# Sparse attention and a gated feed-forward on one core: the first blocks' keys and queries in 1 KB runs, turned by identity matmuls, with constant matmuls in the first waits

## The chip, the core and the metric

The program runs on one core of one Trainium2 chip. A core has a matrix engine (TensorE; PE in the profile, and PEld for its weight loads), a vector engine (VectorE, DVE), a scalar engine (ScalarE, ACT), a general engine (GpSimd, POOL) and a queue engine (SyncE, SP), each with its own stream of instructions, and DMA engines that all queues share. The metric is device time in microseconds of the whole program; lower is better. The median of three runs before the change is 295.51 us (294.74 to 296.17).

## What is computed

Block-sparse causal attention over 4 batches, 8 heads, 768 positions and head size 64, followed by a gated feed-forward over all 3072 tokens. Queries choose the 6 best chunks of 32 keys by an upper bound on their scores.

```python
k_min = np.min(k_chunks, axis=3)
k_max = np.max(k_chunks, axis=3)
ub = np.sum(np.maximum(q[:, :, :, None, :] * k_min[:, :, None, :, :], q[:, :, :, None, :] * k_max[:, :, None, :, :]), axis=-1)
ub = np.where(causal, ub, -1000000000.0)
top_chunks = np.argsort(ub, axis=-1)[..., -top_k:]
scores = scale * np.matmul(q, k.transpose(0, 1, 3, 2))
mask = sel & (pos[:, None] >= pos[None, :])
scores = np.where(mask, scores, -1000000000.0)
...
attn = attn / (np.sum(attn, axis=-1, keepdims=True) + 1e-09)
x = np.ascontiguousarray(attn_out.transpose(0, 2, 1, 3)).reshape(B * S, H * D)
gate = 1.0 / (1.0 + np.exp(-(x @ w_gate)))
val = x @ w_val
return (gate * val @ w_out).astype(np.float32)
```

All inputs are float32; the weights are 512x1536 twice and 1536x512.

## The kernel before

The 24 blocks of 128 rows (6 per batch) are grouped into eight units of three blocks, u0 to u7 (line 659). A first block of a batch can see at most four chunks, so no choice is needed there; the function first (L805) handles those four blocks. Unit 0 is made of the first blocks of batches 0, 1 and 2, and unit 2 takes the first block of batch 3 as its third. For other blocks, keys and queries are turned so that the head dimension lies on partitions; the chunk extremes go into kcr, the bound is formed (ub, L1002), transposed back (ubn), its six largest are found (mx), and the result becomes mask rows beside the queries (ap, apt, hqm), while a fixed pattern beside the keys (epat, copied into hk by the eight hkp operations, L704) turns them into a large negative score. Then come scores (sc), exponential (exp, into four att tiles), causal cut (cm, on GpSimd), product with the values (pv), division (rz, x) and turning (xps, xT).

The feed-forward of a unit (ffn) runs over 12 column blocks fb: g and v products of four matmuls each, a tanh on ScalarE, a combination hg on VectorE; then the output products o in three thirds of the inner dimension, for each of three row blocks. All of g, v and o of all units write one shared key ("ffn"), so their order on TensorE is that in which they are listed: g0, v0, g1, v1 and so on.

A planner (class Plan, L72) fixes the order of the whole program when it is built. Every operation has the engines that can run it with estimated costs, what it reads and writes, and a priority; a list scheduler walks a model of the engines, of buffer slots and of DMA landings. Hand-searched corrections to priorities (NUDGES) and expected landings (LANDS) steer it. What comes out is a static order for each engine: an instruction that waits holds up everything behind it on its engine.

Loads go through SP's queue. For a first block, k and q come in two DMAs each, [128 positions] x [4 heads] x 64 elements (load_first, L731), in 256-byte runs, and v in one. Unit 1's and unit 2's keys and queries come by load_wide, the batches 1 to 3 by load_blocks, values by load_v. The weights are cast to half precision on the way by DMAs that GpSimd issues (weights, L716, and weights_out, L722): wg and wv in three column blocks of 512, then wo in three. The first pair waits for the second q load of block 1; the others are ordered behind the causal cut of block 2.

In first, four PE transposes turn the 128 x 512 tile of k, then of q (L815), into PSUM (kfT, qfT), and one copy each makes half-precision tiles (kf16, qf16). For block 0, chunk minimum and maximum are read from PSUM as well (kxf0, kxf1) and the keys are copied into hk. Scores, exponential, cut, values, division and turning follow per half of the heads (scf, expf, cmf, pvf, rzf, xf, xpsf, xTf).

Buffers named by kind come in a fixed number of slots (np 7, qm 1, ubn 1, att 4, hg 18 and others)[...].

The softmax here doesn't subtract the row's maximum and nothing guards it: scores larger than these inputs give would overflow.

## Time and profile before

| | |
|---|---|
| median of three runs | 295.51 us |
| profiled execution | 295.64 us |
| its span in the trace | 293.94 us |
| mean granted TensorE clock | 0.988 |
| VectorE, ScalarE, GpSimd busy | 189.2, 195.8, 92.5 us |
| HBM read, written | 30.67 MB, 6.29 MB |
| packets under 512 B | 111,424 of 123,233 |

The span runs from the first to the last instruction that the trace records; 1.70 us of the profiled time lie outside it. Busy times of engines overlap, so they don't add up to the span. A line of a timeline gives the start, the time to the end of the last of the merged instructions, engine, source line, operation, output and inputs, shapes and count, and in brackets the idle time before and what ended it. Ends of matmuls are modelled, so for their pace the distance from start to start is used.

### The profile page before, as it was taken

The numbers are of one execution on the slowest core, as the hardware profiler recorded it, in microseconds if no ns is written. First come the engines' busy times: TensorE is split into PE (matmuls) and PEld (weight loads), VectorE is DVE, ScalarE is ACT, GpSimd is POOL, SyncE is SP. The second block draws the span as 40 slices with busy tenths as digits, with TensorE's granted clock in tenths as the row PEclk, the third lists the DMA queues.
The fourth block names the chain that finished last, engine by engine and source line by source line (L and its number), as shares of the span: only waits on it lengthen the run. The fifth ranks groups of instructions, "written<-read, shape, count | busy, mean of one in ns | idle before, by whom it ended". The sixth has DMA issues, their size and how long they took to land.

```text
span 293.9 us, 6954 instructions
## 1 busy us (share of the span) xinstructions
PE 278.2 (95%) x2656; PEld 176.7 (60%) x2656; DVE 189.2 (64%) x560; ACT 195.8 (67%) x398; POOL 92.5 (31%) x162
## 2 busy tenths in 40 slices
PE   2879998999989999999999999999999999999994
PEld 2645555767664566556666667676565557655651
DVE  8375883996999289999999899654134124432420
ACT  7674757977984879458889898886563466323321
POOL 6681314933652337013326954213000011000000
PEclk9977999999999999999999999999999999999999
DMA  7999999999967999399997300001100110011002
GB/s 165 218 249 216 197 197 235 220 146 166 184 100 90 203 188 184 67 215 152 142 210 145 111 3 3 0 2 39 71 2 1 50 60 0 2 38 71 0 15 95
DMA packets 123233, 32.69 MB, mean 111 GB/s; under 512 B 111424, under 2 KB 120128, under 8 KB 123200
## 3 DMA queue, kind: packets, MB, share of 16 engines
q1 hardware_dynamic: 118448, 27.53, 53.1%
q0 software_dynamic: 4752, 4.72, 9.5%
q8 instruction: 21, 0.34, 0.5%
q14 instruction: 12, 0.10, 0.1%
HBM read 30.67 MB, written 6.29 MB: 126 GB/s over the span
## 4 chain that ended last, share of the span: by engine, by line
PE 78%; DMA 10%; DVE 4%; SPq 2%; POOL 2%; ACT 1%; issue 1%; ACTq 0%; DVEq 0%
PE o_u L1168 20%; PE v_u L1146 18%; PE g_u L1146 18%; PE sc_u L1063 11%; DMA wo<-in_moe_w_out_dram 9%; PE pv_u L1096 6%; PE ube_u L1002 2%; SPq L742 2%; PE xps_u L1123 2%; DMA qf<-in_q_dram 1%; DVE qf_u L969 1%; DVE kcr L787 1%; DVE kt L953 1%; ACT attf L857 1%; PE qfT L815 1%
## 5 line engine op out<-in xcount | busy, mean ns | idle before, releaser
L1074 ACT ACTIVATE att_u<-sc_u 128x512 f16<-128x512 f32 (+3 forms) x184 | 88.0, 549 | 13.9 <-PE sc_u L1063 13.1
L1158 DVE SCALAR_TENSOR_TENSOR hg_u<-gate_u,v_u 128x384 f16<-128x384 f16 x96 | 51.8, 544 | 53.8 <-PE v_u L1146 37.0
L1146 PE MATMUL g_u<-xT_u,wg 128*128 128x384 f16 x384 | 79.3, 330 | 0.0
L1146 PE MATMUL v_u<-xT_u,wv 128*128 128x384 f16 x384 | 78.8, 328 | 0.3 <-DMA wv<-in_moe_w_val_dram 0.3
L1154 ACT ACTIVATE gate_u<-g_u 128x384 f16<-128x384 f32 x96 | 47.6, 495 | 39.1 <-DVE hg_u L1158 21.5
L1168 PE MATMUL o_u<-wo,hg_u 128*128 128x512 f16 x288 | 68.0, 379 | 1.1 <-DMA wo<-in_moe_w_out_dram 1.1
L1080 POOL TENSOR_SCALAR_AFFINE_SELECT att_u<-att_u 128x384 f16<-128x384 f16 (+1 forms) x56 | 28.4, 512 | 99.0 <-ACT att_u L1074 98.2
L1146 PEld LDWEIGHTS <-wv 128*128 128x128 f16 x384 | 36.8, 98 | 23.5 <-issue 0.8
L1146 PEld LDWEIGHTS <-wg 128*128 128x128 f16 x384 | 36.5, 99 | 21.8 <-issue 1.5
L1168 PEld LDWEIGHTS <-hg_u 128*128 128x128 f16 x288 | 27.1, 98 | 28.7 <-issue 1.5
L1177 ACT ACTIVATE osb_u<-o_u 128x512 f32<-128x512 f32 x20 | 12.1, 603 | 26.7 <-PE o_u L1168 25.0
L1096 PEld LDWEIGHTS <-att_u 128*128 128x128 f16 x640 | 25.5, 98 | 4.7
L1096 PE MATMUL pv_u<-v,att_u 128*128 128x65 f16 x640 | 28.0, 193 | 0.0
L1063 PE MATMUL sc_u<-hqo,hko 128*128 128x128 f16 (+2 forms) x220 | 27.8, 243 | 0.1
L1063 PE MATMUL sc_u<-hqe,hke 128*128 128x128 f16 (+2 forms) x220 | 27.1, 243 | 0.2 <-ACT att_u L1074 0.2
L1063 PEld LDWEIGHTS <-hke 128*128 128x128 f16 x220 | 16.8, 98 | 5.7 <-issue 1.2
L779 POOL CAST v<-v 128x512 f16<-128x512 f32 x23 | 13.9, 619 | 19.2 <-DMA v<-in_v_dram 18.9
L1063 PEld LDWEIGHTS <-hko 128*128 128x128 f16 x220 | 16.3, 98 | 4.8 <-issue 0.2
L576 DVE COPY xT_u<-xps_u 128x384 f16<-128x384 f16 (+1 forms) x17 | 5.7, 338 | 14.4 <-PE xps_u L1123 14.3
L1115 DVE TENSOR_TENSOR x_u<-pv_u,rz_u 128x384 f16<-128x384 f32 (+1 forms) x28 | 14.5, 523 | 0.4
L1025 DVE MAX8 mx_u<-ubn_u 128x8 f32<-128x8 f32 (+16 forms) x152 | 12.4, 156 | 0.1
L787 DVE TRANSPOSE_TENSOR_REDUCE kcr<-k 128x24 f32<-128x768 f32 x12 | 11.2, 941 | 0.8 <-DMA k<-in_k_dram 0.8
(119 smaller groups left out, 306.9 us busy)
## 6 DMA issues: line engine op xcount, KB each, us to landing
out_dram<-osb_u SPq DMA_DIRECT2D x24, 256.0 KB, 2.4
v<-in_v_dram SPq DMA_DIRECT2D x23, 256.0 KB, 5.0
k<-in_k_dram SPq DMA_DIRECT2D x12, 384.0 KB, 6.1
q<-in_q_dram SPq DMA_DIRECT2D x12, 384.0 KB, 6.8
wg<-in_moe_w_gate_dram POOLq DMA_DIRECT2D x3, 512.0 KB, 10.2
wv<-in_moe_w_val_dram POOLq DMA_DIRECT2D x3, 512.0 KB, 12.8
wo<-in_moe_w_out_dram POOLq DMA_DIRECT2D x3, 512.0 KB, 23.3
kf<-in_k_dram SPq DMA_DIRECT2D x8, 128.0 KB, 3.6
```

The source lines that it names most:

```text
L779: plan.add(f"v16_{b}_{ib}", {POOL: pool(H * D)}, lambda e: nc.gpsimd.tensor_copy(v16[b % 2][:, ib, :, 0:D], at(t)), reads=[t], writes=[("v ...
L787: plan.add(f"kx{m}_{name}_{p}", {DVE: dve(size)}, lambda e, m=m, op=op: nc.vector.tensor_reduce(out=outs[m](), in_=src(), op=op, axis=AX.X ...
L1025: nc.vector.max(at(mx)[:, e_, j, :], at(ubn)[:, e_, j, 0:max(8, u.seen[j])])
L1063: nc.tensor.matmul(at(t)[:, o:o + 128 * m], hk[b % 2][e_][:, p, 128 * jb:128 * jb + 128], hq[u.side][e_][:, p, 128 * x:128 * (x + m)], sta ...
L1074: plan.add(f"exp_{u.name}_{h}_{y}", {ACT: act(n)}, lambda e, t=t, att=att, b0=b0, n=n: nc.scalar.activation(at(att)[:, b0:b0 + n], at(t), ...
L1080: nc.gpsimd.affine_select(out=dv, in_=dv, compare_op=ALU.is_ge, fill=0.0, base=0, pattern=[[0, u.m], [1, 128]], channel_multiplier=-1)
L1096: nc.tensor.matmul(at(pv)[:, last, x, :], at(att)[:, c:c + 128], v16[b % 2][:, jb, h, :], start=(jb == 0), stop=(jb == ib))
L1115: plan.add(f"x_{u.name}_{p}", {DVE: dve(u.t)}, lambda e: nc.vector.tensor_tensor(at(x_).rearrange("p a (e d) -> p e a d", e=2), at(pv)[:, ...
L1146: nc.tensor.matmul(at(t), w16[:, c, 128 * fb:128 * fb + 128], at(u.xt)[:, c, :], start=(c == 0), stop=(c == 3))
L1154: plan.add(f"tanh_{u.name}_{fb}", {ACT: act(T)}, lambda e, g=g, gate=gate: nc.scalar.activation(at(gate), at(g), AF.Tanh, scale=0.5), read ...
L1158: plan.add(f"hg_{u.name}_{fb}", {DVE: dve(T)}, lambda e, w_=w_, gate=gate, hg=hg: nc.vector.scalar_tensor_tensor(at(hg), at(gate), 1.0, at ...
L1168: nc.tensor.matmul(at(o), at(hgs[fc])[:, 128 * tb:128 * tb + 128], wo16[:, fc, :], start=(fc == 0), stop=(fc == NFB - 1))
```

## The change

The planner gets a few additions to its model (landings of a third queue, a limit of eight DMAs in flight, earliest times for single operations in a table HOLDS), and its tables are new: NUDGES and LANDS change throughout, and with them the order on all engines. The rest, cut to its core:

```diff
-        {"ps": 8, "big": 2, "v": 6, "np": 7, "qf": 2, "qm": 1, "kx": 2, "kt": 3, "ubn": 1, "mx": 1, "apt": 1,
-         "att": 4, "rz": 2, "x": 3, "xt": 2, "gate": 4, "hg": 18, "osb": 2},
+        {"ps": 8, "big": 2, "v": 6, "np": 6, "qf": 2, "qm": 1, "kx": 2, "kt": 3, "mx": 1, "apt": 1,
+         "att": 4, "rz": 2, "x": 3, "xt": 2, "gate": 4, "hg": 21, "osb": 2},
...
-                      reads=[epat], writes=[("hkp", i, e_, p) for p in range(o, NP, 2)], prio=0.3 + 0.2 * i, port=True)
+                      reads=[epat], writes=[("hkp", i, e_, p) for p in range(o, NP, 2)], prio=0.7 + 0.8 * i, port=True)
+                later.append((f"hkp{i}{e_}{o}", "g_u0_0" if i == 0 else "g_u1_0"))
+    table = lone("table", [128, 1])
+    const("table", {ACT: (1500, 1600)}, lambda e: nc.scalar.activation(table, ident32[:, 0:1], AF.Exp), reads=["ident32"], prio=-8.5)
...
-                for e_ in range(2):
-                    plan.add(f"{n}f{e_}_{b}", {SP: (450, 450)}, lambda e, t=t[n], src=src, e_=e_: nc.sync.dma_start(
-                        at(t).rearrange("s (p e) d -> s e p d", e=2)[:, e_], heads(src, b, e_)[:, 0:128].rearrange("p s d -> s p d")),
...
+                for g in range(2):
+                    plan.add(f"{n}f{g}_{b}", {SP: (560, 560)}, lambda e, view=view, src=src, g=g: issue(e).dma_start(
+                        view()[:, 256 * g:256 * g + 256], heads(src, b, g)[:, 0:128].rearrange("p (s r) d -> s p (r d)", r=4)),
...
-                for p in range(NP):
-                    nc.tensor.transpose(at(t)[:, p], at(raw[n])[:, 2 * p:2 * p + 2].rearrange("s e d -> s (e d)"), ident32)
+                for r in range(4):
+                    for g in range(2):
+                        c = 256 * g + 64 * r
+                        nc.tensor.matmul(at(t)[ROWS[g], r].rearrange("d s p -> d (s p)"), raw[n][0]()[:, c:c + 64], ident32,
+                                         start=True, stop=True)
...
-            half[n] = Buf("np", f"{n}f16_{b}", [128, NP, 128], F16)
+            half[n] = Buf("np", f"{n}f16_{b}", [128, NP, 128], F16) if b == 3 else Lent(hk[1][b // 2], (0, 1024, 0)[b] + 512 * "kq".index(n), [NP, 128])
...
+                    def chunk(e, m=m, op=op, t=t):
+                        for p in range(NP):
+                            nc.vector.tensor_reduce(
+                                out=at(kx)[:, p] if m else kcr[0][:, p, 0, 0:4],
+                                in_=at(t)[:, :, :, p].rearrange("d r (c s) -> d c s r", c=4), op=op, axis=AX.XY)
...
-        ubn = Buf("ubn", f"ubn_{u.name}", [128, 2, u.nb, 32])
+        ubn = Buf("qm", f"ubn_{u.name}", [128, 2, u.nb, 32])
...
+    warm = ps("warm", "wm", [128, 128])
+    for name, n in {"": 10, "kfT_0": 3, "qfT_0": 3, "kfT_1": 3, "qfT_1": 3, "scf_1": 3, "pvf_0_1": 3, "kfT_2": 3, "qfT_2": 3, "pvf_1_1": 3, "scf_2": 3, "xpsf_1_1": 3}.items():
+        for i in range(n):
+            op = plan.add(f"warm{name}_{i}", pe(213, 170), lambda e: nc.tensor.matmul(at(warm), ident32, ident32, start=True, stop=True),
+                          reads=["ident32"], writes=[warm], prio=1.7)
+            wake.append((op, name))
...
+    gate = [raw_f[1]["v"][1][0]]
+    weights(0, 4, -15.0, gate)
+    weights(4, 8, -1.6, [])
+    weights(8, 12, -1.6, [])
```

In words: a DMA for k or q of a first block now takes four heads and brings four neighbouring rows of one head, 1 KB, to one partition. The partition index is therefore four rows and a head mixed, and eight matmuls with the identity as the moving operand sort it out, 64 columns of the tile at a time; the copy to half precision and the chunk extremes read PSUM in strides, the extremes in eight reductions instead of two. The half-precision tiles, the values and two of the att pairs of batches 0 to 2 have no slots of their own any more: a class Lent gives views into the key and value buffers of batch 1 (hk[1], v16[1]), whose own writers now come after the readers of those views. Block 2's three raw tiles lie in the qm slot. The eight hkp copies are ordered after the start of unit 0's or unit 1's first g product. Forty-three matmuls of the identity with itself write a PSUM tile that nothing reads: ten from the start, and three each that may not start before one of twelve named operations (kfT_0, qfT_0 and so on) has started. ScalarE gets one activation on a constant at the start. The bound turned back (ubn) shares the single qm slot, and the next unit's qm may only start after it. The first pair of weights waits for block 1's v instead of its q; the other weights follow one another with no further wait. Block 3's loads and its first move ahead of unit 2's loads and of unit 1's attention in the planner's list.

## The prediction

> **What bounds the kernel now.** I read the page's busy times and slices first, then a table of windows, then the timeline of TensorE, and last the DMA landings.
>
> ```profile
> PE 278.2 (95%) x2656; PEld 176.7 (60%) x2656; DVE 189.2 (64%) x560; ACT 195.8 (67%) x398; POOL 92.5 (31%) x162
> PE   2879998999989999999999999999999999999994
> PEclk9977999999999999999999999999999999999999
> DMA  7999999999967999399997300001100110011002
> ```
>
> TensorE is busy for 278.2 of 293.94 us, and the slices put its gaps at the two ends. The clock row dips in the third and fourth slice (14.7 to 29.4 us), and the DMA engines are full for the first 11 slices. So the head is where DMA decides, and the rest belongs to TensorE. The windows (columns: window, length, then PE, PEld, DVE, ACT and POOL busy with counts, granted clock, DMA share, GB/s) say how strictly:
>
> ```profile
> 0.00:20.00 20.00, 11.69 (x90) 8.52 (x90) 13.46 (x36) 13.99 (x22) 13.37 (x28) 0.96 1.08 202
> 20.00:48.00 28.00, 25.97 (x181) 15.07 (x179) 18.32 (x61) 17.80 (x40) 8.12 (x14) 0.91 1.19 217
> 48.00:66.00 18.00, 17.60 (x220) 12.13 (x220) 15.67 (x57) 15.12 (x39) 10.86 (x23) 1.00 1.13 190
> 66.00:100.00 34.00, 32.93 (x330) 21.20 (x329) 27.74 (x79) 26.48 (x54) 15.25 (x27) 1.00 0.98 145
> 100.00:180.00 80.00, 80.00 (x925) 52.15 (x923) 72.83 (x230) 65.31 (x132) 34.71 (x55) 1.00 0.85 137
> ```
>
> TensorE idles 8.31 us before 20, 2.03 us from there to 48, 1.47 us from 48 to 100, and not at all from 100 to 180. Its share in the head must also be read with the clock: the finer windows give 0.62, 0.50, 0.50 and 0.67 for the four stretches from 18 to 26 us. The timeline of TensorE shows what ran there:
>
> ```profile
> 4.95 1.09 PE L815 MATMUL kfT<-ident,kf 128*128 128x128 f32 x4 [4.95 <-DMA kf<-in_k_dram]
> ...
> 21.61 1.49 PE L1146 MATMUL g_u<-xT_u,wg 128*128 128x384 f16 x4
> 22.89 1.49 PE L1146 MATMUL v_u<-xT_u,wv 128*128 128x384 f16 x4
> 24.17 1.38 PE L1146 MATMUL g_u<-xT_u,wg 128*128 128x384 f16 x4
> 25.39 0.81 PE L1146 MATMUL v_u<-xT_u,wv 128*128 128x384 f16 x4
> 26.04 0.81 PE L1146 MATMUL g_u<-xT_u,wg 128*128 128x384 f16 x4
> ...
> 29.29 1.24 PE L901 MATMUL qT_u<-ident,qn_u 128*128 128x128 f32 x9
> 30.44 0.55 PE L901 MATMUL kT_u<-ident,kn_u 128*128 128x128 f32 x3
> 31.29 0.82 PE L1146 MATMUL v_u<-xT_u,wv 128*128 128x384 f16 x4 [0.31 <-DMA wv<-in_moe_w_val_dram]
> ...
> 48.09 1.89 PE L1168 MATMUL o_u<-wo,hg_u 128*128 128x512 f16 x8 [1.12 <-DMA wo<-in_moe_w_out_dram]
> ```
>
> The first unit's feed-forward starts at 21.61 us. One product (four matmuls) takes 1.28 us from start to start until 24.17, and 0.65 us from 25.39 on: half clock, then full. Two waits are on weights. From each issue plus its time to landing, the nine weight tiles arrive at 18.4, 22.25, 27.3, 31.2, 34.6, 38.0, 41.4, 44.7 and 48.05 us: wg and wv three times, then wo. The v product of the first third starts 0.6 us after its weights, that of the second as they land, that of the last third at 38.37, 0.4 us after. So up to 48 us the weights pace the feed-forward, and TensorE keeps going by filling in attention work of unit 1.
>
> **What the Trainium skill says.** "TensorE: Matmul & The Clock Gate", section "What's actually happening", says that the clock is half or full and follows the activity of the last 3.4 us window. The trace agrees: the clock record holds 0.5 for 6.83 us, two times 3.41. Its Part 4 says that PE transposes don't count as activity as other matmuls do. No run here separates them, but the half-clock stretch does follow a stretch with many transposes; the change turns by plain matmuls. "DMA: Bandwidth & Descriptors", section "Specifications", puts the smallest run for line rate at 512 B. The page here agrees as far as it goes: 111,424 of 123,233 packets are under 512 B while the head moves about 210 GB/s. "FP8 and Floating Point Precision", section "TensorE Precision Notes", gives true FP32 four passes through the array, which bounds the new turns from above.
>
> **The change part by part.** All from the profiled execution: 295.64 us, of which 293.94 are span and 1.70 lie around it. The median of the runs shown is 295.51, 0.13 below.
>
> *Loads of the first blocks.* The number of SP DMAs stays: 15 for three blocks, some 0.55 us apart on the queue. The 12 for k and q move from 512 packets of 256 B to 128 of 1 KB. Before, time to landing grew from 2.2 us (first) to 4.4 us (fifteenth), so the engines fell behind. Twelve such tiles at the head's rate (128 KB at 210 GB/s is 0.62 us) are 7.5 us of engine time. With longer runs I estimate between nothing and a third saved, 0 to 2.5 us; I take 1.5. It is worth nothing at the very start, where SP's issue then paces, but the following loads, unit 1's k and q (last landing 31.4 us now) and the weights, come that much earlier.
>
> *Weights.* The first one waited for block 1's q and was issued at 10.14. Now it waits for block 1's v, fourteenth on SP: 0.81 + 13 x 0.55 = 8.0 us issue, plus 2.8 to 4.2 us to landing (the bounds are the first loads' 2.2 us and 0.6 for the double size, and the 4.2 of the same load now), gives 10.8 to 12.2. So 0.7 to 2.1 us later at its issue. The second to ninth are no longer held behind the masking of block 2 (the third was issued at 17.07), but that queue is serial, so this buys little. Net of the 1.5 us above I put wo2 between 46.5 and 49.5, taking 47.3.
>
> *Turning.* Eight matmuls of 64 columns replace four transposes per tile. Before, eight transposes at full clock took 0.91 us (60.17 to 61.08). The nearest row to the new form is the bound product, where a group of f32 matmuls over 320 columns starts every 0.29 us, so 128 columns cost about 0.12 us; four passes would be double. A tile costs 0.96 us, up to 1.9, against 0.46. Six tiles lie in the head's idle time. Block 3's two lie where TensorE is full: 2 x 0.96 - 0.91 = 1.0 us lost, up to 2.9.
>
> *Constant matmuls.* 43 of 128x128 f32, between 0.12 and 0.24 us: 5.2 to 10.3 us, against 8.3 us of idle before 20 us plus 0.7 to 22. Placed in waits they are free; above 9.0 us the rest pushes useful work. They are to bring full clock to 21.61 to 25.31, now 3.70 us at half: 1.85 us gained if so, zero if not. At half clock every constant doubles, which is the danger. I take the gain, since every fully busy window in the trace was followed by full clock.
>
> *Unit 1's transposes earlier.* After 21.61 the kernel still turns five tiles of unit 1 (15 matmuls at 0.128, 1.9 us), because their data land late. With loads earlier, some fall in idle time before: 0 to 1.9, I take 1.0. The g and v products can't do this: each writes the shared key of the feed-forward, so g0, v0, g1, v1 keep their order and v0 waits for wv0.
>
> *Stalls.* 1.12 at 48.09 and 0.31 at 31.29: 0 to 1.4 saved, I take 0.6, as block values (v_0_1 to v_0_3) that release unit 1's P·V work are no longer behind as much traffic.
>
> *The eight mask-pattern copies* (hkp) move from 3 to 8 us, where VectorE and ScalarE waited for data, to the start of g of unit 0 and of unit 1. They cost 0.55 us each on VectorE, 1.47 on ScalarE. The first four have cover (VectorE is busy 18.3 of 28 us there); the last four land where VectorE is at 72.8 of 80. At most 2.2 us of VectorE, zero for TensorE as long as ready feed-forward work covers it.
>
> *With one answer:* lent tiles and batch 1's wait for their readers (these end near 20 us, batch 1's keys come after 60) cost nothing; neither does ubn in qm's single slot, since the next unit's qm comes 15 us later and is held until then; the minimum and maximum in 8 strided pieces cost VectorE some 0.9 us in its 4.34 us wait before 13.47; the table activation on ScalarE lies before its first data.
>
> Sum: -1.85 - 1.0 - 0.6 + 1.0 = -2.45; 295.64 - 2.45 = 293.2.
>
> **Rivals.** *Absorbed:* the head gains, but TensorE then catches up with VectorE and ScalarE, which are at 85% in 48 to 66 us and VectorE at 91% in 100 to 180, with 2.2 us of copies more. For: those shares. Against: no idle on TensorE in 100 to 180, thus ready work in hand. The gain shrinks to 0.2: 295.4. *Weights later:* the new gate delays the whole weight queue, and TensorE, having used up what it may fill in (four att tiles, values not in), waits at each third of the feed-forward and at wo. Place: v0, v of fb 4 and 8, wo2. It decides once wg0 is issued after about 12.5 us; at 13.5 us, less the 1.5 won, wo2 comes 1.9 later, and with no fill gained and block 3's 1.0 that is +2.9: 298.5, and at 12.5, 297.5; I put 298. For: fourteenth in the queue; against: less DMA time ahead of it. *Clock not held:* the change doesn't do what it says. Constants at half clock, 43 x 0.24 or more = 10.3 us in the 9.0 of idle time, delay the chain by 1.3 at least and win back nothing; with block 3's 1.0 it is 297.9.
>
> **How the numbers follow.** Forecast 50%, absorbed 20%, weights later 22%, clock not held 8%. The forecast's own range is 291.0 to 294.6, from the ends above (another 0.9 of transposes, 0.8 of stalls and a little of the weights; or no transposes moved). Taking in the two slower cases the range is 290.8 to 298.5. About 0.5%, 1.5 us, is what a measurement here can tell from no change: faster is below 294.0, slower above 297.0. The forecast gives 0.48 of faster and a little of same; the absorbed case is nearly all same; the last two are slower: 0.49, 0.22, 0.29.
>
> **What would show it.** Clock 1.00 from 10 us on and g, v at 0.65 from the first product; unit 1's transposes before 22 us; weights landing as put; no wait on wo; TensorE still at 80 of 80 in 100 to 180. Wrong if wg0 is issued after 12.5 us, if constants sit between useful matmuls after 22 us, if a turn costs over 1.5 us, or if TensorE idles after 100 us.

## The result, and the profile after

The changed kernel takes 306.46 us (median, 303.11 to 309.71), the kernel before, run beside it, 295.84 (294.74 to 296.82). The ratio is 1.033, with a 95% interval from 1.026 to 1.040: 10.6 us slower by the medians and 9.8 by the ratio, where 2.4 us faster was forecast. A run more than 1.5% above the fastest of its kernel is counted as slow: the ratios below leave it out and the medians don't, and it concerns one run each of the changed kernel (309.71), of the first order moved by hand (314.39, the run that was traced) and of the last run below (304.89). The profiled execution took 306.82 us with a span of 305.1, so the two traces differ by 11.2 us of span.

First the page of the changed kernel, the rows that were read of the kernel before:

```profile
PE 289.2 (95%) x2838; PEld 189.7 (62%) x2838; DVE 189.1 (62%) x566; ACT 191.0 (63%) x395; POOL 97.1 (32%) x166
PE   7939999999989979999999999999999999999994
PEclk9997999999999999999999999999999999999999
DMA  5999999579999999969994340001100010001002
```

TensorE is as full as before (95%), and it is busy 11.0 us longer. The clock is better: full in the first three slices, and low only in the fourth. The DMA row has a new hole in its eighth and ninth slices (53 to 69 us, "57"): SP's queue stands from 51.84 to 61.97 behind the store of unit 0's first output, with batch 1's keys behind it, so the late head delays the next loads too. Busy time alone would suggest that the added matmuls are the whole cost. The groups of the page price them:

```profile
L1334 PE MATMUL warm<-ident 128*128 128x128 f32 x86 | 15.2, 314 | 1.7 <-POOL ident masks.py:199 1.7
```

The 43 constants are 86 records, two each, 15.2 us with their overlap. But a busy TensorE that multiplies constants is not a TensorE at work, and whether it would have had other work to do is read from the windows and the timeline. The windows of the changed kernel (columns as before):

```profile
0.00:20.00 20.00, 15.21 (x179) 13.22 (x179) 7.68 (x26) 8.98 (x16) 10.37 (x23) 1.00 0.85 195
20.00:48.00 28.00, 24.68 (x207) 19.01 (x208) 20.06 (x67) 17.86 (x40) 8.45 (x15) 0.94 1.20 228
48.00:66.00 18.00, 18.00 (x200) 12.53 (x199) 12.11 (x36) 13.86 (x34) 7.47 (x17) 1.00 0.77 132
66.00:100.00 34.00, 32.23 (x360) 20.47 (x359) 31.81 (x104) 27.13 (x55) 19.39 (x33) 1.00 1.19 158
100.00:180.00 80.00, 78.46 (x801) 49.73 (x806) 67.00 (x184) 58.84 (x122) 35.13 (x54) 1.00 1.02 138
```

Up to 20 us VectorE does 7.68 us of work where it did 13.46, and ScalarE 8.98 for 13.99. So the head's real work, of which those two do a part, is behind by 20 us already. TensorE has also lost its unbroken stretch from 100 to 180 (78.46 of 80). The timeline of TensorE shows by how much the head is late:

```profile
23.32 0.88 PE L1016 MATMUL qT_u<-ident,qn_u 128*128 128x128 f32 x3 [3.90 <-DVE rzf L987]
...
30.73 0.49 PE L1016 MATMUL qT_u<-ident,qn_u 128*128 128x128 f32 x3
31.06 0.81 PE L1264 MATMUL g_u<-xT_u,wg 128*128 128x384 f16 x4
31.71 0.49 PE L1016 MATMUL qT_u<-ident,qn_u 128*128 128x128 f32 x3
32.04 0.83 PE L1334 MATMUL warm<-ident 128*128 128x128 f32 x6
32.71 0.81 PE L1264 MATMUL v_u<-xT_u,wv 128*128 128x384 f16 x4
33.36 0.81 PE L1264 MATMUL g_u<-xT_u,wg 128*128 128x384 f16 x4
```

The first feed-forward product starts at 31.06 instead of 21.61. Full clock is there (0.65 us from product to product), and so are six constant records between two useful products. The weights are not what it waited for: the first landed at 18.5. It waited for its input, the outputs of blocks 0 to 2, and those waited for their divisions (rzf). The first row shows TensorE's own part: it stood 3.90 us in front of a turn of unit 1's queries, with block 2's products behind it in its queue. What that turn reads is a copy made on VectorE at 22.62, which ended within 0.1 us of the division that the row names. VectorE and ScalarE of the changed kernel (rows picked; a bracket holds the idle time of the engine ahead of the row, and what ended it):

```profile
17.12 0.55 DVE L660 COPY kn_u<-kq_u 128x384 f32<-128x384 f32 x1 [1.46 <-DMA kq_u<-in_k_dram]
20.54 0.55 DVE L660 COPY kn_u<-kq_u 128x384 f32<-128x384 f32 x1 [2.87 <-DMA kq_u<-in_k_dram]
22.62 0.55 DVE L660 COPY qn_u<-kq_u 128x384 f32<-128x384 f32 x1 [1.33 <-DMA kq_u<-in_q_dram]
23.09 0.17 DVE L987 RECIPROCAL rzf<-pvf 128x4 f32<-128x4 f32 x1
23.59 0.51 ACT L658 COPY kn_u<-kq_u 128x384 f32<-128x384 f32 x1 [4.74 <-DMA kq_u<-in_k_dram]
```

and the same operations in the kernel before, again picked:

```profile
13.47 0.18 DVE L872 RECIPROCAL rzf<-pvf 128x4 f32<-128x4 f32 x1 [4.34 <-PE pvf L866]
15.05 0.24 DVE L872 RECIPROCAL rzf<-pvf 128x4 f32<-128x4 f32 x2
15.41 0.51 ACT L574 COPY kn_u<-kq_u 128x384 f32<-128x384 f32 x1 [0.23 <-DMA kq_u<-in_k_dram]
15.93 0.17 DVE L872 RECIPROCAL rzf<-pvf 128x4 f32<-128x4 f32 x1
17.74 0.17 DVE L872 RECIPROCAL rzf<-pvf 128x4 f32<-128x4 f32 x1
18.99 0.18 DVE L872 RECIPROCAL rzf<-pvf 128x4 f32<-128x4 f32 x1 [0.30 <-PE pvf L866]
```

Before, VectorE divides as soon as each block's product is there and leaves unit 1's copies to ScalarE. After, three of unit 1's copies stand at the head of VectorE's in-order queue, each waits for a load, and a division that takes 0.17 us runs at 23.09, though its product had ended by 18.5. The planner put them there because its table of landings told it that these loads would be in early. From the LANDS tables of the two programs, in us of the planner's clock, and from the traces, when the first reader ran:

| load | planned before | first reader before | planned after | first reader after |
|---|---|---|---|---|
| unit 1, first keys read | 14.2 | 15.4 | 12.8 | 17.1 |
| unit 1, first queries read | 22.2 | 23.9 | 14.4 | 22.6 |
| batch 0, values 3 | 45.5 | 48.6 | 40.7 | 49.3 (landed at 42.2) |
| batch 1, last keys | 67.7 | 72.1 | 65.6 | 76.9 |

The new tables expect these loads 1 to 8 us earlier than the old ones, and no reader reads its load earlier by as much. The third row is not a late load, though. These values landed at 42.2 (issued at 24.09, 18.1 us to landing), 6.3 us earlier than before and 1.6 after the plan. Their reader on GpSimd stood behind causal cuts that waited for ScalarE, and waited for no load:

```profile
48.80 0.52 POOL L1201 TENSOR_SCALAR_AFFINE_SELECT att_u<-att_u 128x384 f16<-128x384 f16 x1 [0.53 <-ACT att_u L1195]
49.27 0.61 POOL L884 CAST v<-v 128x512 f16<-128x512 f32 x1
```

The weights had meanwhile become later: GpSimd, which issues them, waited for copies of unit 1 and sent the third pair of wg and wv at 28.22 instead of 19.18.

How the lateness grows can be estimated from the traces. Count the matmul records that have started by a given time, without constants and first blocks' turns, and give each the usual distance from its start to the next start at full clock. By this count TensorE of the changed kernel is 7.8 us of work behind the kernel before at 40 us, 7.1 at 80, 8.3 at 100, 10.3 at 120 and 10.9 at 200. So most of the loss is made in the head. Another 2 us come at 110.8, when keys of batch 2 land for which VectorE stands 5.30 us; on ScalarE a cast of these keys stands in front of the exponentials that TensorE then waits for:

```profile
110.84 1.84 DVE L892 TRANSPOSE_TENSOR_REDUCE kcr<-k 128x24 f32<-128x768 f32 x2 [5.30 <-DMA k<-in_k_dram]
112.10 0.45 PE L1217 MATMUL pv_u<-v,att_u 128*128 128x65 f16 x9 [1.40 <-ACT att_u L1195]
```

That readers planned too early for their loads are the loss became the theory to test, beside the obvious rivals: the constants, and the new loads with their turns.

### The profile page after: what moved, and what is told of

The parts are those of the page before. It is cut to its first block, busy times and chain, and to the rows that moved or that the text cites. A ratio compares the mean times of both kernels' runs of the same rounds, so it can differ in the third digit from the quotient of the medians.

```text
span 305.1 us, 7343 instructions
## 1 busy us (share of the span) xinstructions
PE 289.2 (95%) x2838; PEld 189.7 (62%) x2838; DVE 189.1 (62%) x566; ACT 191.0 (63%) x395; POOL 97.1 (32%) x166
## 4 chain that ended last, share of the span: by engine, by line
PE 76%; DMA 8%; SPq 7%; ACT 3%; DVE 3%; issue 1%; ACTq 0%; DVEq 0%
PE o_u L1303 19%; PE v_u L1264 17%; PE g_u L1264 17%; PE sc_u L1184 9%; PE pv_u L1217 5%; DMA kq_u<-in_q_dram 3%; DMA q<-in_q_dram 3%; SPq L868 2%; SPq L847 2%; PE ube_u L1123 2%; PE warm L1334 2%; DMA k<-in_k_dram 2%; ACT att_u L1195 2%; PE xps_u L1244 1%; DVE hg_u L1284 1%
## 5 line engine op out<-in xcount | busy, mean ns | idle before, releaser
L1264 PE MATMUL g_u<-xT_u,wg 128*128 128x384 f16 x384 | 78.1, 326 | 0.3 <-ACT gate_u L1277 0.2
L1312 ACT ACTIVATE osb_u<-o_u 128x512 f32<-128x512 f32 x23 | 13.8, 598 | 32.0 <-PE o_u L1303 31.9
L1217 PEld LDWEIGHTS <-att_u 128*128 128x128 f16 x640 | 24.8, 98 | 5.8 <-ACT att_u L1195 1.7
L1217 PE MATMUL pv_u<-v,att_u 128*128 128x65 f16 x640 | 27.0, 193 | 1.4 <-ACT att_u L1195 1.4
L1184 PEld LDWEIGHTS <-hko 128*128 128x128 f16 x220 | 16.9, 98 | 7.1 <-issue 1.0
L1334 PE MATMUL warm<-ident 128*128 128x128 f32 x86 | 15.2, 314 | 1.7 <-POOL ident masks.py:199 1.7
L892 DVE TRANSPOSE_TENSOR_REDUCE kcr<-k 128x24 f32<-128x768 f32 x12 | 11.2, 949 | 5.3 <-DMA k<-in_k_dram 5.3
L1334 PEld LDWEIGHTS warm<-ident 128*128 128x128 f32 x86 | 12.8, 217 | 2.4 <-POOL ident masks.py:199 1.7
## 6 DMA issues: line engine op xcount, KB each, us to landing
wv<-in_moe_w_val_dram POOLq DMA_DIRECT2D x3, 512.0 KB, 10.8
```

The lines of the kernel that those rows point to most:

```text
L1184: nc.tensor.matmul(at(t)[:, o:o + 128 * m], hk[b % 2][e_][:, p, 128 * jb:128 * jb + 128], hq[u.side][e_][:, p, 128 * x:128 * (x + m)], sta ...
L1217: nc.tensor.matmul(at(pv)[:, last, x, :], at(att)[:, c:c + 128], v16[b % 2][:, jb, h, :], start=(jb == 0), stop=(jb == ib))
L1264: nc.tensor.matmul(at(t), w16[:, c, 128 * fb:128 * fb + 128], at(u.xt)[:, c, :], start=(c == 0), stop=(c == 3))
L1312: nc.scalar.activation(at(osb), at(o), AF.Copy, scale=0.5) if e == ACT
L1334: op = plan.add(f"warm{name}_{i}", pe(213, 170), lambda e: nc.tensor.matmul(at(warm), ident32, ident32, start=True, stop=True), reads=["id ...
```

## The experiments

Medians and 95% intervals are of rounds beside the kernel before, which lay between 295.1 and 295.9 us in all batches.

**No constants.** All 43 constant matmuls are left out, the order of the rest stays.

```diff
     for op in plan.order():
+        if op.name.startswith("warm"):
+            continue
         op.emit(op.engine)
```

> The changed kernel without its 43 constant matmuls, all else and the order of everything else unchanged. Theory W (waits): copies of unit 1 that wait for late loads stand in VectorE's, ScalarE's and TensorE's queues ahead of the first blocks' divisions, and so hold the first feed-forward until 31 us; then g of unit 0 starts at 26 to 28 us instead of 31.06 and the time falls by 3 to 5 us to 301 to 303. Theory C (constants): the constants themselves hold TensorE's queue; then g starts at about 22 us and the time falls by 9 us or more, to 297 or less. Theory T (turning and loading): the new loads and turns made the first blocks late; then g stays within 1 us of 31 and the time within 2 us of 306.5.

Measured: 303.5 us, ratio 1.024 (1.019 to 1.030). The constants cost 2 to 3 us net here by ratios and medians (the two intervals overlap), and about 8 remain. The first product starts at 25.95, at half clock. The theory of the waits is 0.5 us off in the time; that of the constants is ruled out as the whole of the loss.

**Unit 1's copies don't wait.**

```diff
-            e, at(nat), at(u.raw)[:, j, p].rearrange("p h x d -> p x h d")),
+            e, at(nat), ident32.rearrange("p (h d) -> p h d", h=2).unsqueeze(1).to_broadcast([128, m, 2, D]) if u.i == 1
+            else at(u.raw)[:, j, p].rearrange("p h x d -> p x h d")),
```

> The changed kernel with the eight copies of unit 1's keys and queries reading the identity tile instead of the loaded tile (same shape and number of copies; the loads are still issued; unit 1's attention is therefore computed from other data). So nothing waits for unit 1's loads, while all orders and all 43 constants stay. W: g of unit 0 starts at 21 to 23.5 us and the time falls by 7 to 9 us, to 297.5 to 299.5. C: g starts at 29 us or later and the time falls by 2 us at most. T: no change within 2 us.

Measured: 304.63 us, ratio 1.032 (1.027 to 1.038). A miss. The first product came at 23.99, 7.1 us earlier, and only 1.8 us of it by the medians, 0.3 by the ratios, reached the end. GpSimd's timeline in this run shows where it went, at the casts of batch 0's later values:

```profile
44.41 0.62 POOL L884 CAST v<-v 128x512 f16<-128x512 f32 x1 [6.04 <-DMA v<-in_v_dram]
44.98 1.47 POOL L1202 TENSOR_SCALAR_AFFINE_SELECT att_u<-att_u 128x384 f16<-128x384 f16 x3
48.38 0.61 POOL L884 CAST v<-v 128x512 f16<-128x512 f32 x1 [1.94 <-DMA v<-in_v_dram]
```

The last values land at 48.3, as they do in the kernel before (48.6), and 6 us later than in the changed kernel. There the third pair of weights left at 28.22, here at 19.95, so the freed head also sent the weights out earlier, ahead of these values; that this is what delayed the values is likely, but no run isolates it. And here unit 1's products with the values stand in front of unit 0's output products in TensorE's fixed order, so TensorE stood for 3.3 of the 6 us from 44 to 50, and ran at half clock from 48.1 to 54.9. The first store of unit 0 left at 61.28, 0.7 us ahead of the changed kernel's.

**Unit 1's copies moved by hand** behind the first blocks' divisions and between the feed-forward products, slots given out anew for that order, with the constants and then without them:

```diff
...
+    LATE = {'kn_u1_2': 'xTf_1_0', 'qn_u1_1': 'v_u0_0', 'kn_u1_0': 'g_u0_1', 'qn_u1_2': 'v_u0_1', 'qn_u1_3': 'v_u0_2', 'qn_u1_0': 'g_u0_4', 'kn_u1_3': 'g_u0_4'}
...
```

> The changed kernel with only the order of the head edited: the copies of unit 1's keys and queries (and what depends on them) come behind the first blocks' chain and between the first feed-forward products, at the places where their loads have landed in the trace; buffer slots are handed out again for this order. Constants stay. W: g of unit 0 starts at 21 to 23 us, v by 24, and the time falls by 6 to 8 us, to 298.5 to 300.5, less than without any wait, since constants of the old waits still stand between products. C: g starts at 27 us or later, the time falls by 3 us at most. T: no change within 2 us.

> The same order as in the order experiment, and no constant matmul. If waits and constants both cost: 9 to 11 us below the changed kernel, 295.5 to 297.5, so within 0.5% of the kernel before. If the constants only bring clock and cost nothing: slower than the order experiment by 1 to 2 us, with a granted clock of 0.5 for some 7 us around the first products.

Measured: 309.01 us, ratio 1.044 (1.038 to 1.049), and 308.09, ratio 1.043 (1.038 to 1.048). Both miss, on the slow side. One of the eight copies (kn_u1_1) was left in its place. With constants the one trace has the first product at 29.84. Without them it starts at 23.0, but between 20 and 48 TensorE is busy for only 20.26 of 28 us: the moved transposes now wait between the products. A place chosen by hand only moved the wait here, as everything behind it kept its order.

**The kernel before with constants, and with free loads.** Two controls on the other side: constants in front of waiting products of the head (17 by the edit, though the recorded texts say 21), and the loads of unit 1 and of batch 0's later values not waited for.

```diff
...
             def values(e, e_=e_, pv=pv):
+                for _ in range(CONST.get(f"pvf_{b}_{e_}", 0)):
+                    nc.tensor.matmul(at(pv).rearrange("s p d -> s (p d)")[:, 0:128], ident32, ident32, start=True, stop=True)
                 for p in range(NP):
...
```

> The kernel before with 21 constant products with the identity put in front of products of the head that wait (1 each before the first block's waiting output product of block 1, 4 each for block 2, 2, 2 and 3 before unit 1's key transposes), its order else the same. The prediction's clock term alone: 1.85 us less, 293.7 (292.8 to 294.5), full clock from 5 to 40. If the constants only fill waits and the clock was not what limits the head: 295.6 within 0.7. If they delay the work behind them: 296.5 or more.

> The kernel before with the same edit as the first run of this batch (unit 1's copies and the casts of batch 0's later values read the identity). Theory P: its order was laid out for unit 1's loads landing at 14 to 28 and the last values at 45.5, which is where they land, so little is waited for: 1 to 3 us less, 292.5 to 294.5. If it gains 6 us or more, waits for these loads weigh as much in the kernel before as after, and P does not explain the difference between the two.

Measured: 294.96 us, ratio 1.000 (0.998 to 1.002), and 294.86, ratio 1.000 (0.998 to 1.001). Both equal the kernel before; the second misses its range by 0.4 us. With the constants the head has the clock that the prediction wanted. The two windows up to 48 us of that run:

```profile
0.00:20.00 20.00, 13.22 (x116) 10.97 (x117) 13.66 (x36) 14.09 (x23) 13.92 (x28) 1.00 1.09 203
20.00:48.00 28.00, 25.58 (x193) 15.44 (x192) 18.35 (x63) 18.73 (x42) 8.62 (x16) 1.00 1.20 220
```

and its wait for the output weights:

```profile
46.93 1.89 PE L1174 MATMUL o_u<-wo,hg_u 128*128 128x512 f16 x8 [1.24 <-DMA wo<-in_moe_w_out_dram]
```

Its products run 0.65 us apart from the first at 21.19, and then TensorE still waits 1.24 us for the last third of wo, as before (1.12). The clock in the head was worth nothing, net of what 17 constants cost. Runs without any constant say the same: of 69 runs of the kernel before, beside all versions, seven had a mean clock of 0.999 or more, with a median of 295.4 us, and 28 had less than 0.990, with a median of 295.5. And the kernel before loses nothing by unit 1's loads and batch 0's values: its order has other work in front of whatever reads them.

**All of it free in the changed kernel, step by step.** First unit 1's copies and the casts of batch 0's values; then without constants; then also unit 2's copies and block 3's turns and values. The edit is of the kind shown above.

> The changed kernel in which unit 1's eight key and query copies and the three casts of batch 0's later values read the identity instead of the loaded tiles (the loads are still issued; all that follows from unit 1's keys, queries and batch 0's last values is computed from other data). Theory P, the order was laid out for landings that come 5 to 9 us too late, and the values are the second such landing after the keys and queries: both waits are gone, the first feed-forward product starts at 22 to 24.5, TensorE does not idle between 44 and 49.5 (1.7 of 4 and 1.0 of 4 us idle there when only the keys and queries were freed), the output of unit 0 leaves by 56, and the time is 297 (294 to 300). Rival R, the loss is in what TensorE has more to do (constants, turns) and not in waits: the time stays at 303 to 305.

> As the run before, and the 43 constant products are left out besides. Theory P: with no load to wait for, the constants no longer stand in idle time but in front of work, so leaving them out gains more than the 3 us that it gained in the changed kernel itself: 291 to 295, 3 to 6 us below the run before. Rival R: the constants are the loss itself: about 8 to 10 us below the run before. Third possibility C: they keep the clock up as much as they cost: within 1 us of the run before.

> The changed kernel in which, besides unit 1's copies and the casts of batch 0's later values, unit 2's copies, block 3's turns and block 3's value copy read the identity (loads still issued; everything that follows is computed from other data). In the run that freed unit 1 and the values alone TensorE stood 2.1 us before 49.81 for block 3's keys, planned for 41.8. Theory O: that wait goes as well, and 298 to 300 is left, of which about 2 us are new idle time of TensorE between 66 and 115 (3.0 us there against 1.1 in the kernel before) and the rest constants and turns. If the time stays at 301 to 303, block 3's wait is only moved.

Measured: 301.82 us, ratio 1.022 (1.018 to 1.026); 303.01, ratio 1.024 (1.019 to 1.030); 300.73, ratio 1.020 (1.016 to 1.024). The first misses the range of the wait theory by 1.8 us. The reason is of the same kind as in the run with free copies. TensorE's timeline of the first of these runs:

```profile
47.43 0.27 PE L1185 MATMUL sc_u<-hqe,hke 128*128 128x256 f16 x1
49.81 0.41 PE L922 MATMUL kfT<-ident,kf 128*64 128x128 f32 x2 [2.10 <-DMA kf<-in_k_dram]
```

The values no longer hold anything up, and block 3's keys do: planned for 41.8, they land at 49.7 in this run (43.4 in the changed kernel, where the weights are later). Freeing these as well left 5.4 us, 0.7 more than expected. The constants cost 2 to 3 us in the changed kernel, and here leaving them out saved nothing (the intervals overlap), against the 3 to 6 expected: with them the clock stays full over the waits, without them it fell to a mean of 0.91 between 48 and 66.

**Loads and turns alone, on either side.** In the changed kernel the first blocks' loads and turns are put back as they were; in the kernel before they are put in, without and with the 17 constants.

```diff
-                        view()[:, 256 * g:256 * g + 256], heads(src, b, g)[:, 0:128].rearrange("p (s r) d -> s p (r d)", r=4)),
+                        view().rearrange("s (p e d) -> s e p d", p=NP, e=2)[:, g], heads(src, b, g)[:, 0:128].rearrange("p s d -> s p d")),
...
-                for r in range(4):
-                    for g in range(2):
-                        c = 256 * g + 64 * r
-                        nc.tensor.matmul(at(t)[ROWS[g], r].rearrange("d s p -> d (s p)"), raw[n][0]()[:, c:c + 64], ident32,
-                                         start=True, stop=True)
+                for p in range(NP):
+                    nc.tensor.transpose(at(t)[:, p], raw[n][0]()[:, 128 * p:128 * p + 128], ident32)
```

> The changed kernel with one part undone: the first blocks' keys and queries are loaded in the runs of the kernel before and turned by its four transposes of 128 columns a tile; order, tiles and constants stay. Theory O, the loss sits in the new order, laid out for loads that land later than it assumes: only the dearer turns come back (kfT and qfT take 9.8 us of TensorE here and 7.8 in the kernel before), partly hidden in the head: 304 to 306.5. Rival T, the turns and the slower issue of the 1 KB loads are the loss: 301 or less.

> The kernel before with that part alone: the first blocks' keys and queries come in 1 KB runs and are turned by eight products with the identity a tile; order and tiles stay those of the kernel before. Theory O: block 3's turns cost about 1 us, those of the first three blocks are mostly hidden, 295.5 to 297. Rival T: the loss comes with the loads and turns, 299 or more. If the earlier landing of the first tile is worth something by itself: below 294.5.

> As the run before, with the 21 constant products added that cost nothing in the kernel before (ratio 1.000 there): everything that the change is called for, in the order of the kernel before. Theory O: as the run before within 0.7 us, so that some 9 us of the changed kernel's 10.6 belong to its order. Rival T: 300 or more.

Measured: 304.6 us, ratio 1.031 (1.027 to 1.036); 297.07, ratio 1.006 (1.004 to 1.009); 298.05, ratio 1.009 (1.005 to 1.012). This tells the theories apart. Put into the old order, the loads and turns cost 1.8 us (0.1 over the expected range), and with constants 2.8 (0.3 more than the 0.7 allowed beside the run without). Taken out of the new order, the loads and turns give back 1.9 of the 10.6 us by the medians, 0.5 by the ratios. So most of the loss came with the order and what is built into it (next runs).

**The order alone**, that is old loads and turns and no constants in the changed kernel, and then without the waits for batch 0's loads, and then for batch 1's keys. What stays beside the order are the lent tiles, the new slot counts, the moved mask copies and the new grouping of the weights; no run separates these from it. The line that frees batch 1's key casts:

```diff
...
-                     lambda e, p=p, k16=k16: copy(e, at(k16), at(raw)[:, p]), reads=every, writes=[k16], prio=next_())
+                     lambda e, p=p, k16=k16: copy(e, at(k16), ident32[:, 0:CH].unsqueeze(1).to_broadcast([128, NC, CH]) if b == 1 else at(raw)[:, p]), reads=every, writes=[k16], prio=next_())
...
```

> The changed kernel with the old loads and turns and without the constants: what stays is the new order, the weights of four blocks at a time and the lent tiles. Theory O: the constants gained 3 us when left out of the changed kernel, so 301.5 (300 to 303), about 6 us above the kernel before, all of it order. Rival S, the order is dear only because constants and turns crowd it: 298 or less.

> As the run before, and unit 1's and unit 2's copies, block 3's turns and value copy, and the casts of batch 0's later values read the identity (loads still issued; what follows is computed from other data). Theory O: the waits for batch 0's late loads are 3 to 4 us of it and the rest is idle time of TensorE after 66: 297 to 299. If the same 301 to 303 comes out, waits for loads are not what the order loses without constants, and it is lost in the later stages.

> As the run before (order alone, batch 0's loads not waited for), and batch 1's key casts and chunk extremes read the identity as well (what follows from batch 1's keys is computed from other data). In the run before, TensorE led the kernel before by 1.5 to 2.6 us of work up to 66, then ScalarE's cast of batch 1's keys waited 3.4 us for the load that landed at 72.4 with an exponential and a gate behind it, TensorE stood 2.4 us, and by 80 the lead was a lag. Theory O (each late load is the next wait in line): 2.5 to 4 us less, 297 to 298.5. If it stays at 300 to 302, the lag after 66 has another cause than that load.

Measured: 303.19 us, ratio 1.023 (1.019 to 1.028); 301.21, ratio 1.020 (1.017 to 1.023); 301.94, ratio 1.018 (1.009 to 1.026). The order alone costs 5.6 to 8.3 us (0.2 over the expected range by the median). Freeing loads gains little, a miss twice over: both times the recorded alternative was measured, that the loss then lies elsewhere, in later stages. The timelines show where, and what waits there are again readers of late loads. In the second run the head is no longer late: the first product starts at 23.06, and in work done, counted as above, TensorE is 1.9 us ahead of the kernel before at 66 us. At 80 it is 1.9 behind. ScalarE and TensorE there:

```profile
72.42 0.83 ACT L658 CAST k<-k 128x768 f16<-128x768 f32 x1 [3.39 <-DMA k<-in_k_dram]
73.16 0.48 ACT L1275 ACTIVATE gate_u<-g_u 128x384 f16<-128x384 f32 x1
73.54 1.56 ACT L1193 ACTIVATE att_u<-sc_u 128x512 f16<-128x512 f32 x3
```

```profile
73.69 0.39 PE L1182 MATMUL sc_u<-hqe,hke 128*128 128x256 f16 x2 [2.44 <-ACT gate_u L1275]
```

Batch 1's last keys land at 72.3, and ScalarE's cast of them stands ahead of a gate and three exponentials. In the kernel before they land at 71.9, and its ScalarE has the gate and, in the rows left out, three exponentials from 72.09 on in front of the cast:

```profile
71.70 0.49 ACT L1154 ACTIVATE gate_u<-g_u 128x384 f16<-128x384 f32 x1
...
73.58 0.83 ACT L574 CAST k<-k 128x768 f16<-128x768 f32 x1
```

The third run frees the keys, and at 72 us leads by 2.2 us of work and at 80 by 1.0. Then batch 1's queries are next, first on VectorE and through it on TensorE:

```profile
84.44 2.28 DVE L1088 STREAM_TRANSPOSE qf_u<-q 128x384 f32<-128x384 f32 x5 [4.84 <-DMA q<-in_q_dram]
```

```profile
87.22 0.74 PE L1121 MATMUL ube_u<-qf_u,kcr 64*32 64x320 f32 x1 [2.98 <-DVE hg_u L1282]
```

The clock fell with it, to half from 86.4 to 93.2:

```profile
80.00:100.00 20.00, 17.01 (x144) 8.90 (x142) 12.57 (x52) 8.13 (x16) 7.35 (x12) 0.83 1.19 162
```

That is 3.0 us idle (1.0 in the kernel before) and 3.4 us lost to the clock, and it accounts for the whole change from 1.0 ahead at 80 to 4.1 behind at 100. The kernel before turns these queries with no wait ahead:

```profile
85.15 2.24 DVE L969 STREAM_TRANSPOSE qf_u<-q 128x384 f32<-128x384 f32 x5
```

There the last of them had landed at 81.3, here it landed at 84.3. So up to about 90 us these kernels move at the pace of loads that come in one order through SP's queue, and the orders differ in whether there is other work in front of each reader. The estimate of the work that TensorE has done, less that of the kernel before, in us:

| version | at 40 | 60 | 80 | 100 | 120 | 200 |
|---|---|---|---|---|---|---|
| changed kernel | -7.8 | -7.8 | -7.1 | -8.3 | -10.3 | -10.9 |
| unit 1's copies don't wait | -0.8 | -7.0 | -6.4 | -7.2 | -7.2 | -8.5 |
| order alone | -4.8 | -4.0 | -3.3 | -4.1 | -5.1 | -7.6 |
| and batch 0's loads free | 0.8 | 1.6 | -1.9 | -2.5 | -3.5 | -4.2 |
| and batch 1's keys free | 1.1 | 1.9 | 1.0 | -4.1 | -4.0 | -5.0 |

The last column agrees within 0.3 us with the differences of the spans.

No version that ran beats the kernel before.

## Why the prediction was wrong

The step that failed is *Unit 1's transposes earlier* (-1.0), with the assumption under the whole sum that each edit's cost can be added to the old order, so that the new order of all engines was put at nothing. The step took it that unit 1's loads land earlier and let their readers move up. They do not land earlier: the first of them landed at 17.1 us (15.3 before), the first queries at 22.6 (22.5), the last at 30.9 (31.5). The readers did move up, ahead of the first blocks' divisions on VectorE and their products on TensorE, and took the chain with them: the first feed-forward product came at 31.06 instead of 21.61, and with these copies freed of their loads at 23.99. In place of -1.0 the order, with what is built into it, costs 5.6 to 8.3 us by itself. The early readers are shown as the cause of the late head, 7.8 us of work at 40 us against 0.8 without them. How much of the 5.6 to 8.3 us is theirs at the end is not isolated, since freeing them alone let later waits take their place. The diff shows the new LANDS, and setting them against the landings in the trace of the kernel before would have told of it; the prediction passed over them.

The other terms:

- *Clock* (-1.85): the mechanism was right and the value wrong. Constants hold the clock full (1.00 up to 23.0 us, and through the whole head in the kernel before with constants), but in the old order it is worth 0 within 0.6 us. The weights land when they land, and the wait for wo stays at 1.24. This is the rival *absorbed*, only with the weights as what absorbs, not VectorE and ScalarE. In the changed kernel the clock then fell anyway, between 23.0 and 26.4, behind the wait.
- *Constant matmuls*, taken as free inside 9.0 us of idle time: they took 15.2 us and 2 to 3 us of the time. There are ten at the start and three each at eleven operations, not twelve. Each is about 0.22 us at full clock (two records, 0.112 apart), 9.6 us for 43, near the upper of the bounds of 5.2 and 10.3: an fp16 score product of the same size starts every 0.056 us, so the four passes of the upper bound are what the trace shows. The rest is overlap of records and the half-clock stretch. The sign that the prediction named as showing it wrong, constants between useful matmuls after 22 us, is what the trace shows.
- *Turning* (+1.0): right in size, and in part by luck. Block 3's two tiles take 1.90 us (54.96 to 56.86, and 1.92 predicted). Each turn is two records, as the doubled bound had it, but the records start in pairs 7 ns apart, one pair every 0.1 us, and the two cancel. Loads and turns together cost 1.8 us in the old order, which would leave 0.8 us for the first three blocks, whose turns the prediction put into idle time.
- *Loads of the first blocks* (1.5 us of engine time saved): a 1 KB load lands in 2.5 to 3.3 us, where k and q took 2.2 to 4.3, but an issue in this head takes 0.60 us on SP, not 0.50. The last load of these blocks is issued at 9.83, not 9.31, and lands at 14.8, about 1 us later than before. The packets' time was saved: with the new loads alone in the old order the DMA engines' busy share over the first 20 us is 0.87, not 1.08. It did not reach what follows, as unit 1's first load landed there at 16.9 instead of 15.3 us and its last at 30.6 instead of 31.5.
- *Weights* and the rival *weights later*: I gave the gate on block 1's v an issue at 10.8 to 12.2. The first weight load left at 10.56, some 3.5 us before that v is in: the gate is an edge in the planner and no wait in the program. The first four landings, 18.5 to 30.6, are within 0.7 us of before. From the fifth on they are later, and wo2 landed at 50.0, 1.9 us after the 48.05 of before, because GpSimd sent the third pair only at 28.22. So the rival had the right sign and even its 1.9 us, but not by the gate, and TensorE, later still, never waited for these weights.
- *Stalls* (-0.6): batch 0's values did land earlier, as the term had it (31.7 to 42.2 us, where it was 38.2 to 48.6), and the wait on wo is gone, because TensorE comes to its first output product 10 us late (53.67 instead of 43.55). Neither gained time.
- *Mask copies, lent tiles, strided extremes*: nothing in the runs speaks against the zero given to them, but none isolates them; they are inside the "order alone".

If the parts may be added at all, 2.8 us for loads, turns and constants in the old order (there 17 constants, not 43) and 5.6 to 8.3 for the new order make 8.4 to 11.1, around the 9.8 to 10.6 that were measured. What stays open is how fast this order would be if planned on the landings that the trace shows. Its tables of priorities and earliest times are fitted to the early landings, and a new fit was not tried. The runs that freed one load after another show a next wait each time, in traces whose loads had moved as well. They don't show that an order with all loads met would be faster than the kernel before, nor what the lent tiles and slots in it cost.

## What to carry to other kernels

When a change brings a new static order, compare what the order assumes with what the trace shows before adding up the edits: list the assumed landing of every load beside its measured one, and ask of each early reader what stands behind it on its in-order engine. Divisions of 0.17 us behind waiting copies put the head 7 us behind here. Tell a late load from a late reader by the landing itself. And the head, paced by loads, gave nothing back for a faster clock and little for a removed wait: free one load, look for the next wait, and look at which transfers now start earlier, before counting the gain.

## What the runs showed that I had not expected

- A plain f32 matmul appears as two records: 86 for 43 constants of 128 columns, 0.112 us apart at full clock; the turns of 64 columns run two side by side, 0.06 us a record on average.
- With the first blocks' loads in 1 KB runs SP takes longer for each issue, 0.60 against 0.50 us, though they have a quarter of the packets. It is not these loads' shape alone: the v loads among them, unchanged, also take 0.59 us instead of 0.51.
- With its waits filled by constants the version with freed keys, queries and values keeps full clock where without them it has half clock twice, so leaving out 43 useless matmuls saved 2 to 3 us in the changed kernel and none there (301.82 with, 303.01 without).
- A wait can cost about as much again in clock: TensorE's waits of 2.44 and 2.98 us in the last two runs were followed by 3.4 and 6.8 us at half clock. A wait of 3.69 us in the run of the order alone was not.
- The changed kernel scattered more over its four runs (303.1 to 309.7) than the kernel before (294.7 to 296.8). No run here says why.
